# New planned durations and a new order for a planned f32 attention and two-MLP kernel

## The chip, the core and the metric

The kernel runs on one core of a Trainium2 chip. Its engines are TensorE (PE, with weight loads PEld beside it), VectorE (DVE), ScalarE (ACT), GpSimd (POOL) and SyncE (SP), which issues DMAs. The metric is the device time of one execution in microseconds (us).

## The reference

For 4 batches of 12 heads (448 tokens, 64 elements), all in f32:

```python
q_n, k_n = rmsnorm(q, g_q), rmsnorm(k, g_k)          # over head_dim
scores = q_n @ k_n.T / sqrt(64)
attn = exp(scores - max(scores)); attn /= sum(attn) + 1e-9
x = (attn @ v) as [1792, 768]
h = x @ w_in1;  x = (h * sigmoid(1.702 * h)) @ w_out1        # 768 -> 2048 -> 768
h = x @ w_in2;  out = (h * clip(h + 3, 0, 6) / 6) @ w_out2   # 768 -> 2048 -> 768
```

## The kernel before

TensorE has to deliver f32 accuracy, so nearly every operand is cut into a 16-bit "high" part and a 16-bit "low" part, and a product is made of two or three 16-bit products of 128x448. Making these parts is the work of the other engines: `scaled` (L479 ScalarE, L482 VectorE, L485 GpSimd) writes high parts, `rest` (L494, VectorE) and `split` (L509 GpSimd, L510 VectorE) low parts. Weights arrive as f32 and are decoded (L613 to L634) and split too.

The stages overlap. Per batch: squares and root of the norms (L971 to L1018), norm products (L1028), high and low parts of q and k (L1034 to L1049), a transposition by DMA, then per pair of heads seven score tiles in groups of one or two. A score group is a chain over four engines: score products (L1203, L1206) into one of two PSUM buffers `s`, row maxima (L1211, VectorE), their scaling to the exponentials' bias (L1215, ScalarE, 128x2), the exponentials with row sums (L1216, ScalarE), the sums' scaling (L1221, ScalarE, 128x2), the reciprocals (L1224, VectorE). The exponentials release the `s` buffer. In batch 0 the probabilities are scaled through a diagonal matrix (L485 on GpSimd, 128x128) and turned by TensorE (L1265), in the later batches they are split and turned by DMA. The products with v are L1131 (batch 0) and L1164. MLP 1 follows for each batch: inward products L1410 (16 column blocks `f`, 18 products each), gate, L1459 (VectorE), split, then outward products L1478. MLP 2 (seven products in the place of eight: L1654 and L1769) comes last, for all batches.

No loop order is written out. Every operation is recorded in a plan with its dependencies, buffers and its ways: `op([(POOL, ns, f), (DVE, ns, g)], deps)` may run on either engine. `Plan.rank` gives each the longest planned path to the end (plus hand-set offsets `off` and `own`), `Plan.order` then lists all operations by planned start; where there are several ways it takes the engine with the earliest planned end plus a bias (`bias0` in batch 0, `bias1` in batch 1, `bias` after). The planned durations come from small functions such as `t_pe(n) = 0.445 * n`. On the chip each engine runs its own instructions in this fixed order and waits by semaphores; a planned time is only a way to an order. `keep_busy` (L319) puts filler products (L1959, 128x512 bf16, results unused) where the plan sees TensorE idle for longer than `late + idle` ns.

In `add_in` the inward products of `f >= 2` also wait for `kg_ready`, which needs the largest x of the batch (a total over partitions, the TensorE product L444).

Of the kernel before, what the change touches and what calls it, by code (L numbers as in the profile page):

```python
# [9 lines left out]
F16 = mybir.dt.float16  # L10
# [32 lines left out]
    look=[0, 130, 60, 920, 540],  # L43
    off=[-9158, 408922, -29895, 22854, 24586, 19810, -27690, 67476, -181023, 15083, 120686, -34408, -37087, -37194, -689989, -31399, -23083, -347804, 11747, 208998],
    abias=44617,
    cuts=[],
    bias0=[2000, 440, 370, 120, 3040],
    bias1=[8820, 1540, 3900, 3250, 4520],
    dlook=2054,
    warm=9,  # L50
    late=789,
    idle=1000,
    pu=419,
    pmost=5,
# [25 lines left out]
def t_pe(n):  # L80
    return 0.445 * n
# [14 lines left out]
def t_fast(n):  # L96
    return Shared(0.72 * n + 80)


def t_dve_two(n):  # L100
    return Shared(1.04 * n + 150)


def t_dve_rest(n):
    return Shared(1.04 * n + 205)


def t_dve_bits(n):
    return Shared(1.04 * n + 150)


def t_pool(n):
    return Shared(0.78 * n + 290)


def t_pool2(n):
    return Shared(1.5 * n + 380)
# [212 lines left out]
def attention_moe_moe_kernel(ctx, tc, q, k, v, g_q, g_k, w_in1, w_out1, w_in2, w_out2, out):  # L330
# [181 lines left out]

    gp, gq_t = sb.tile([128, D], F32, name="gp"), vr_t[0][:, 0, :]
    gm, ge, tab = small(), small(), small()
    alpha, nalpha = small(), small()
# [4 lines left out]
    SLOTS0 = 10  # L520
    pt0 = carve(arena, 0, [128, 10, 4, 128], F32)

    def constants():
        nc.gpsimd.memset(one, 1.0)
        make_identity(nc, ident)
# [35 lines left out]
    class Weight:  # L561
# [22 lines left out]
        def decoded(self, src, raw, cl):  # L584
# [69 lines left out]
        def add(self, i, m, after):  # L654
# [3 lines left out]
            for j in range(i, i + m):  # L658
# [9 lines left out]
                squares.append(op((ACT, t_act(n, 1) + 45, square), [o] + after))  # L668
# [13 lines left out]
            o = op((DVE, 480 if self.inward else 550, scale), [o], gives=wl)  # L682
# [53 lines left out]
    class Units:  # L736
# [8 lines left out]
        def add(self, q, after, free):  # L745
# [7 lines left out]
            for j in range(2):  # L753
# [63 lines left out]
                squares.append(op((ACT, t_act(n, 1) + 45, square), [o], gives=raw))  # L817
# [71 lines left out]
    msq, rsq, tsq, nbs, zs = small(56), small(56), small(56), small(16), small(16)  # L889
# [53 lines left out]
    def add_norm(bt, after):  # L943
# [75 lines left out]

        def put(n, raw, rooted, gained):  # L1020
# [59 lines left out]
        for grp in groups:  # L1080
# [3 lines left out]
                (DVE, 2300, lambda n=grp[0], m=m: root(n, m)), sum((p[1] for p in parts), [])  # L1084
# [53 lines left out]
    def add_pair(bt, n):  # L1138
# [4 lines left out]
        for p0, j0, t0, m in ((0, 0, 0, 7), (64, 0, 1, 6), (64, 6, 0, 1)):  # L1143
            def load(p0=p0, j0=j0, t0=t0, m=m):
# [3 lines left out]
                128 * m * 256, load, loads[:1] or [bt.vscale] + batches[0].pvs, takes=None if loads else raw_l, wide=False  # L1148
# [20 lines left out]
    def add_units(bt, exp_after, arena_after, x_after):  # L1169
        b = bt.b  # L1170
        bt.xlow, bt.pvs, xmax = [], [], []
        x_factor = 2.0 ** -14 if b else bt.xf
        nslots = 12 if b else SLOTS0
        reads = [arena_after] * nslots
        ring = 0
        u = 0
        rows = lambda h: slice(64 * h, 64 * h + 64)
        for n in range(NP):
            groups = [(0, 1), (2, 3), (4, 5), (6,)] if n % 2 == 0 else [(0,), (1, 2), (3, 4), (5, 6)]
            slots = [(ring + i) % nslots for i in range(7)]  # L1180
            ring += 7
            turns = [None] * 7
# [6 lines left out]
            for grp in groups:  # L1189
                m = len(grp)  # L1190
                sl, pl, hl = Lease(s_ring, m), [Lease(p_ring) for _ in grp], Lease(phl_ring) if b else None
# [21 lines left out]
                def exps(i, sl=sl, nb=nb, z=z, p=p, m=m):  # L1213
                    if i == 0:
                        nc.scalar.activation(out=nb, in_=nb, func=AF.Copy, scale=nalpha)  # L1215
                    nc.scalar.activation(  # L1216
                        out=p(i), in_=s_t[sl.slot][:, i, :S], func=AF.Exp, bias=nb[:, i:i + 1],
                        scale=alpha, accum_out=z[:, i:i + 1],
                    )
                    if i == m - 1:  # L1220
# [786 lines left out]
```

## Time and profile before

| | us |
|---|---|
| median of 3 runs (lowest, highest) | 1145.58 (1145.24, 1148.97) |
| the profiled execution | 1147.63 |
| its span | 1145.8 |
| TensorE busy | 1065.3 (93%) |
| VectorE busy | 822.5 (72%) |
| ScalarE busy | 721.3 (63%) |
| GpSimd busy | 365.1 (32%) |

In the profile's strip of 40 slices TensorE stands at 8 or 9 tenths everywhere but at the start (3) and in one stretch at 129 to 193 us (6, 4 and 4 tenths), and the granted clock falls there to 5 tenths. VectorE stands at 7 to 9 tenths up to there. The DMA engines move 156 GB/s on average. A window of the trace gives for each engine its busy us in that stretch; a row of waits names the engine and line that waited and the instruction whose end released it.

### The profile page before, as it was taken

The numbers are of one execution on the slowest core, as the hardware profiler recorded it, in microseconds if no ns is written. First come the engines' busy times: TensorE is split into PE (matmuls) and PEld (weight loads), VectorE is DVE, ScalarE is ACT, GpSimd is POOL, SyncE is SP. The second block draws the span as 40 slices with busy tenths as digits, with TensorE's granted clock in tenths as the row PEclk, the third lists the DMA queues.
The fourth block names the chain that finished last, engine by engine and source line by source line (L and its number), as shares of the span: only waits on it lengthen the run. The fifth ranks groups of instructions, "written<-read, shape, count | busy, mean of one in ns | idle before, by whom it ended". The sixth has DMA issues, their size and how long they took to land. (4 is left out here: it accounts for less than half of the span.)

```text
span 1145.8 us, 18018 instructions
## 1 busy us (share of the span) xinstructions
PE 1065.3 (93%) x6571; PEld 588.7 (51%) x6571; DVE 822.5 (72%) x1445; ACT 721.3 (63%) x1505; POOL 365.1 (32%) x335
## 2 busy tenths in 40 slices
PE   3888964999999999999999999999999999999998
PEld 1566531554554555545555555555555555555555
DVE  7998889998699764797756878594577455935342
ACT  5999758999868996578885646463565132512210
POOL 6764555353156201350001255552132103200000
PEclk9999985999999999999999999999999999999999
DMA  8977578999976997569895327633451151222033
GB/s 239 193 199 192 167 203 212 204 191 222 241 227 187 173 176 155 181 194 166 171 185 154 120 78 264 231 108 120 146 189 55 56 169 40 71 72 98 1 90 104
DMA packets 236712, 178.88 MB, mean 156 GB/s; under 512 B 194896, under 2 KB 220496, under 8 KB 235088
## 3 DMA queue, kind: packets, MB, share of 16 engines
q1 hardware_dynamic: 236624, 177.74, 59.4%
q8 instruction: 51, 0.84, 0.3%
q14 instruction: 37, 0.30, 0.1%
HBM read 97.88 MB, written 34.41 MB: 115 GB/s over the span
## 5 line engine op out<-in xcount | busy, mean ns | idle before, releaser
L1410 PE MATMUL mm<-xt,wa 128*128 128x448 f16 x1152 | 229.5, 357 | 7.0 <-DVE st L1459 6.8
L1478 PE MATMUL mm<-gt,wb 128*128 128x448 f16 x1152 | 226.7, 352 | 0.7 <-DVE wb L494 0.5
L1769 PEld LDWEIGHTS <-gt 128*128 128x128 f16 x1344 | 131.4, 98 | 92.3 <-issue 4.8
L1410 PEld LDWEIGHTS <-wa 128*128 128x128 f16 x1152 | 113.9, 100 | 114.3 <-issue 14.5
L1478 PEld LDWEIGHTS <-wb 128*128 128x128 f16 x1152 | 111.8, 99 | 103.9 <-issue 1.1
L1654 PEld LDWEIGHTS <-xt 128*128 128x128 f16 x1008 | 98.6, 98 | 93.7 <-issue 3.8
L1216 ACT ACTIVATE p<-s,smalls 128x448 f32<-128x448 f32 x168 | 120.7, 720 | 7.5 <-DVE p L494 3.4
L1654 PE MATMUL s<-wa,xt 128*128 128x448 f16 x576 | 114.1, 352 | 2.1 <-DVE st L1669 2.1
L1211 DVE TENSOR_REDUCE smalls<-s 128x2 f32<-128x896 f32 (+1 forms) x96 | 91.5, 963 | 4.1 <-PE s L1206 3.9
L494 DVE SCALAR_TENSOR_TENSOR p<-p,smalls 128x448 f16<-128x448 f32 x108 | 78.1, 752 | 22.4 <-ACT p L479 22.1
L1203 PE MATMUL s<-gt 128*128 128x448 f16 (+1 forms) x192 | 62.2, 370 | 30.2 <-ACT p L1216 28.3
L1654 PE MATMUL mm<-wa,xt 128*128 128x448 f16 x432 | 86.9, 352 | 0.9 <-ACT wb L1676 0.9
L479 ACT ACTIVATE p<-p,smalls 128x448 f16<-128x448 f32 (+2 forms) x120 | 75.8, 666 | 11.7 <-DMA xt<-p 8.6
L1769 PE MATMUL mm<-p,gt 128*128 128x384 f16 x384 | 72.0, 326 | 0.0
L1769 PE MATMUL mm<-gt 128*128 128x384 f16 x372 | 68.2, 326 | 0.0
L1206 PE MATMUL s<-gt 128*128 128x448 f16 (+1 forms) x192 | 61.9, 366 | 0.0
L1769 PE MATMUL s<-p,gt 128*128 128x384 f16 x288 | 56.1, 326 | 2.4 <-ACT wb L1805 1.2
L1769 PE MATMUL s<-gt 128*128 128x384 f16 x300 | 55.9, 326 | 1.0 <-DVE st L1669 0.6
L494 DVE SCALAR_TENSOR_TENSOR gt<-st,smalls,gt 128x448 f16<-128x448 f32 x64 | 52.4, 829 | 6.1 <-ACT gt L479 4.9
L1808 DVE SCALAR_TENSOR_TENSOR wb<-mm,smalls,wb 128x384 f32<-128x384 f32 x47 | 27.0, 611 | 41.0 <-PE mm L1769 41.0
L479 ACT ACTIVATE gt<-st,smalls 128x448 f16<-128x448 f32 x49 | 32.1, 661 | 29.9 <-DVE st L1459 26.2
L1265 PE MATMUL mm<-gt,p 128*128 128x128 f32 x336 | 44.1, 280 | 6.3 <-DVE xt L1276 1.9
(216 smaller groups left out, 1827.4 us busy)
## 6 DMA issues: line engine op xcount, KB each, us to landing
wr<-in_moe_w_in_dram SPq DMA_DIRECT2D x32, 768.0 KB, 4.9
wa<-park_x SPq DMA_DIRECT2D x21, 672.0 KB, 4.0
wr<-in_moe_w_out_dram SPq DMA_DIRECT2D x12, 1024.0 KB, 6.4
wr<-in_moe_w_out_dram SPq DMA_DIRECT2D x16, 768.0 KB, 4.7
qkd<-xt SPq DMA_DIRECT2D x18, 672.0 KB, 4.7
p<-in_v_dram SPq DMA_DIRECT2D x42, 224.0 KB, 4.1
x2d<-st SPq DMA_DIRECT2D x24, 224.0 KB, 3.1
park_x<-wa SPq DMA_DIRECT2D x2, 2688.0 KB, 13.0
```

What stands on the lines that cost most here:

```text
L479: nc.scalar.activation(out=dst(), in_=src(), func=AF.Copy, scale=s)
L494: nc.vector.scalar_tensor_tensor(out=dst(), in0=src(), scalar=s, in1=high(), op0=ALU.mult, op1=ALU.subtract)
L1203: nc.tensor.matmul(o, lhsT=x[:, 64 * t:64 * t + m], rhs=x[:, 448:896], start=True, stop=False)
L1206: nc.tensor.matmul(o, lhsT=x[:, 64 * t:64 * t + m], rhs=x[:, 896:1344], start=False, stop=True)
L1211: nc.vector.tensor_reduce(out=nb, in_=s_t[sl.slot][:, :m, :S], axis=AX.X, op=ALU.max)
L1216: nc.scalar.activation(out=p(i), in_=s_t[sl.slot][:, i, :S], func=AF.Exp, bias=nb[:, i:i + 1], scale=alpha, accum_out=z[:, i:i + 1],)
L1265: nc.tensor.matmul(mm_t[tl.slot][:, 128 * j:128 * j + 128], lhsT=p(i)[:, c:c + 128], rhs=diag(), start=True, stop=True,)
L1410: nc.tensor.matmul(mm_t[ml.slot][:, :n], lhsT=w.inw(we, kc, f), rhs=x[:, xe, kc, :n], start=(kc == k0 and i == 0), stop=(kc == k1 - 1 and ...
L1478: nc.tensor.matmul(mm_t[ml.slot][:, :S], lhsT=W2.outw(we, fc, d * 128, 128), rhs=gv[:, ge_, fc, :], start=(fc == g.part.start and i == 0), ...
L1654: nc.tensor.matmul(self.bank(k), lhsT=w[:, we, fa, kc], rhs=xs[:, fb, xe, kc], start=first and kc == 0 and j == 0, stop=kc == 2 and j == 2 ...
L1769: nc.tensor.matmul(mm_t[banks[h].slot][:, :half], lhsT=g[:, ge, f, tb * 128:tb * 128 + 128], rhs=w4_t[part % 2][:, f, we, h * half:h * hal ...
L1808: nc.vector.scalar_tensor_tensor(out=view(), in0=bank(), scalar=self.co, in1=view(), op0=ALU.mult, op1=ALU.add)
```

## The change

The arithmetic of the output is the same. Changed are the numbers that the plan goes by, and a few operations' ways.

- Planned durations: TensorE products 0.445 to 0.4225 ns a column, the total over partitions 420 to 150, the batch-0 products with v 2400 to 4290; the fast VectorE form 0.72n+80 to 0.57n+75, VectorE's two-input, `rest` and 16-bit forms 55 to 72 ns shorter, GpSimd's two-input form 120 ns shorter; some scalings longer.
- The scalings at L1215 and L1221 are no longer part of the exponentials' operation. Each is an operation of its own with three ways, ScalarE, GpSimd or VectorE (L1280, L1282, L1284 and L1295, L1297, L1299 of the new file).
- The root of the norms gets a way on GpSimd; the new order never takes it. New code for `plain` and `defer` is there, with values that leave the old computation; one small memset is added.
- All tuning numbers (`bias`, `off`, `own`, `late` 789 to 500, `idle` 1000 to 900, ...) are new, so the order is planned anew.

```diff
-    bias0=[2000, 440, 370, 120, 3040],
-    bias1=[8820, 1540, 3900, 3250, 4520],
+    bias0=[10940, 1120, 970, 600, 5420],
+    bias1=[8440, 0, 13700, 2530, 6480],
-    late=789,
-    idle=1000,
+    late=500,
+    idle=900,
...
 def t_pe(n):
-    return 0.445 * n
+    return 0.4225 * n
 def t_fast(n):
-    return Shared(0.72 * n + 80)
+    return Shared(0.57 * n + 75)
 def t_dve_two(n):
-    return Shared(1.04 * n + 150)
+    return Shared(1.04 * n + 80)
 def t_pool2(n):
-    return Shared(1.5 * n + 380)
+    return Shared(1.5 * n + 260)
...
-        o = op((PE, 420, emit), deps, takes=lease)
+        o = op((PE, 150, emit), deps, takes=lease)
...
-                    if i == 0:
-                        nc.scalar.activation(out=nb, in_=nb, func=AF.Copy, scale=nalpha)
...
+                o = op([
+                    (ACT, 265, lambda nb=nb, late=late: nc.scalar.activation(
+                        out=nb, in_=nb, func=AF.Copy, scale=nalpha, bias=UP if late else 0.0)),
+                    (POOL, 510, lambda nb=nb, late=late: nc.gpsimd.tensor_scalar(
+                        out=nb, in0=nb, scalar1=nalpha, scalar2=UP if late else 0.0, op0=ALU.mult, op1=ALU.add)),
+                    (DVE, 150, lambda nb=nb, late=late: nc.vector.tensor_scalar(
+                        out=nb, in0=nb, scalar1=nalpha, scalar2=UP if late else 0.0, op0=ALU.mult, op1=ALU.add)),
+                ], [o])
...
-                        (ACT, t_act(S, 3) + 200 * (i == 0) + 160 * (i == m - 1), lambda i=i, f=exps: f(i)),
+                        (ACT, t_act(S, 1 if late else 3) - 35, lambda i=i, f=exps: f(i)),
...
-                o = op((PE, 12 * t_pe(S) + 700, both_heads), deps[0] + deps[1] + vdone, takes=ml, gives=vl)
+                o = op(
+                    (PE, (19 if late else 12) * t_pe(S), both_heads), deps[0] + deps[1] + vdone,
+                    takes=[ml, zl] if late else ml, gives=vl,
+                )
...
-                o = op((PE, 2400, both), deps[0] + deps[1], takes=ml, gives=vls[0])
+                o = pv_done = op((PE, 4290, each_head), deps[0] + deps[1], takes=ml, gives=vls[0])
```

What the new order does is read at three places. The new file's lines are 10 to 91 higher: L1071, L1092, L1089, L504, L1261, L1501, L454 and L2050 are before's L1028, L1049, L1046, L494, L1216, L1410, L444 and L1959.

The first is VectorE in the norms of batch 1, before:

```order
L494 SCALAR_TENSOR_TENSOR gt<-p,smalls,gt 128x7x64
L1028 TENSOR_TENSOR xt<-xt,smalls 128x448 x2
L494 SCALAR_TENSOR_TENSOR gt<-p,smalls,gt 128x7x64
L1046 TENSOR_TENSOR xt<-xt 128x7x64
L1049 TENSOR_TENSOR xt<-xt 128x7x64
L459 TENSOR_SCALAR smalls<-mm_74 128x1
```
and now:

```order
L1071 TENSOR_TENSOR xt<-xt,smalls 128x448 x2
L1092 TENSOR_TENSOR xt<-xt 128x7x64
L1071 TENSOR_TENSOR xt<-xt,smalls 128x448
L1089 TENSOR_TENSOR xt<-xt 128x7x64 x2
L504 SCALAR_TENSOR_TENSOR gt<-p,smalls,gt 128x7x64
L1092 TENSOR_TENSOR xt<-xt 128x7x64
```
Norm products and low parts (`xt` on both sides) that GpSimd did before stand here on VectorE.

The second is ScalarE in the first score groups of batch 0 (`s` is the score buffer, `smalls` holds maxima and sums), before:

```order
L1215 ACTIVATE smalls<-smalls 128x2
L1216 ACTIVATE p,smalls<-s_75,smalls 128x448 x2
L1221 ACTIVATE smalls<-smalls 128x2
L479 ACTIVATE gt<-gt,smalls 128x128
L613 ACTIVATE wr<-wr 128x768
L1034 ACTIVATE gt<-wb 128x896
L1275 COPY xt<-mm_73 128x512
L1215 ACTIVATE smalls<-smalls 128x2
L1216 ACTIVATE p,smalls<-s_76,smalls 128x448
```
ScalarE now, without the 128x2 rows:

```order
L1261 ACTIVATE p,smalls<-s_75,smalls 128x448 x2
L685 ACTIVATE wa,smalls<-wb 128x6x128
L1261 ACTIVATE p,smalls<-s_76,smalls 128x448 x2
L685 ACTIVATE wa,smalls<-wb 128x6x128
L1261 ACTIVATE p,smalls<-s_75,smalls 128x448 x2
L946 ACTIVATE p,smalls<-p 128x448
L1261 ACTIVATE p,smalls<-s_76,smalls 128x448
```
and GpSimd at the same place, where the rows L1282 and L1297 are those scalings:

```order
L495 TENSOR_SCALAR gt<-wb 128x7x64
L1089 TENSOR_TENSOR gt<-wb,gt 128x7x64
L1282 TENSOR_SCALAR smalls<-smalls 128x2
L1092 TENSOR_TENSOR gt<-wb,gt 128x7x64
L1282 TENSOR_SCALAR smalls<-smalls 128x2
L1297 TENSOR_SCALAR smalls<-smalls 128x2
L495 TENSOR_SCALAR gt<-gt,smalls 128x128
L1297 TENSOR_SCALAR smalls<-smalls 128x2
L495 TENSOR_SCALAR gt<-gt,smalls 128x128 x2
```
They are queued between the large parts of k and q (`gt<-wb`) and the diagonals (L495).

The third is TensorE in batch 0's inward products, where the total that `f >= 2` waits for is made, before (`mm` are PSUM tiles, `wa` the weights):

```order
L1410 MATMUL mm_71<-xt,wa 128x448
L1410 LDWEIGHTS wa
L1410 MATMUL mm_71<-xt,wa 128x448
L444 MATMUL mm_74<-smalls 128x1
L1410 LDWEIGHTS wa
L1410 MATMUL mm_72<-xt,wa 128x448
```
and now, where the pair of L2050 stands 58 times in a row, and the inward products of `f >= 2` behind it:

```order
L1501 LDWEIGHTS wa
L1501 MATMUL mm_72<-xt,wa 128x448
L454 MATMUL mm_73<-smalls 128x4
L2050 LDWEIGHTS ident_70
L2050 MATMUL mm_74<-ident_70 128x512
```
Where TensorE's queue went straight on to the next column block, fillers stand now. In the whole program the fillers go from 36 to 124. By the order, VectorE has 1580 instructions (1447 before), ScalarE 1150 (1207), GpSimd 278 (340); GpSimd has 53 of the 192 small scalings (44 of them before the first outward product of batch 0), VectorE 10. Before the first outward product of batch 0, TensorE has 170 score products where it had 156.

## Rows read from the trace of the kernel before

**Rows 1.** Windows: busy us of each engine by stretch, granted clock; they overlap.
```profile
core 0: us, PE busy (x) PEld busy (x) DVE busy (x) ACT busy (x) POOL busy (x), PEclk, DMA share, GB/s
0.00:25.00 25.00, 5.51 (x14) 2.04 (x15) 17.05 (x41) 13.00 (x28) 14.59 (x22) 1.00 0.80 229
25.00:238.00 213.00, 174.87 (x1149) 105.37 (x1150) 194.65 (x355) 182.52 (x421) 123.00 (x119) 0.93 0.79 199
129.00:193.00 64.00, 37.49 (x182) 17.54 (x181) 56.02 (x108) 44.80 (x87) 35.41 (x29) 0.78 0.77 211
238.00:316.00 78.00, 73.77 (x528) 39.94 (x527) 62.05 (x125) 72.17 (x164) 25.61 (x23) 1.00 0.92 218
316.00:722.00 406.00, 398.29 (x2514) 209.20 (x2513) 303.50 (x540) 296.62 (x659) 123.74 (x111) 1.00 0.72 176
722.00:1146.00 424.00, 412.89 (x2375) 232.16 (x2373) 245.25 (x386) 156.96 (x237) 78.19 (x63) 1.00 0.31 100
```

**Rows 2.** Waits of TensorE from 129 to 193 us: total, times, longest.
```profile
PE s L1203 <- ACT p L1216: 14.7, 4, 4.9
PE mm L1410 <- DVE st L1459: 6.5, 2, 5.8
PE mm L444 <- ACT p L1216: 5.1, 1, 5.1
```

**Rows 3.** VectorE by line and shape, 0 to 238 us: count, busy us, mean ns.
```profile
L1211 DVE TENSOR_REDUCE smalls<-s 128x2 f32<-128x896 f32 x28 | 29.9, 1077 | 0.1
...
L494 DVE SCALAR_TENSOR_TENSOR p<-p,smalls 128x448 f16<-128x448 f32 x13 | 12.7, 996 | 0.5 <-ACT p L479 0.5
...
L634 DVE SCALAR_TENSOR_TENSOR wr<-wr 128x1024 int32<-128x1024 int32 x6 | 8.8, 1464 | 0.3 <-ACT wr L613 0.3
...
L1028 DVE TENSOR_TENSOR xt<-xt,smalls 128x448 f32<-128x448 f32 x5 | 5.1, 1060 | 0.0
L494 DVE SCALAR_TENSOR_TENSOR wb<-wr,smalls,wb 128x1024 f16<-128x1024 f32 x4 | 5.1, 1269 | 0.0
L628 DVE TENSOR_SCALAR wr<-wr 128x1024 uint16<-128x1024 uint16 x6 | 4.5, 743 | 0.0
...
L1046 DVE TENSOR_TENSOR xt<-xt 128x448 f16<-128x448 f32 x2 | 2.1, 1034 | 0.0
...
L510 DVE TENSOR_TENSOR p<-p 128x448 f16<-128x448 f32 x1 | 1.4, 1449 | 0.0
```

**Rows 4.** Timeline of VectorE from 147 to 150 us: start, duration.
```profile
147.73 1.15 DVE L1028 TENSOR_TENSOR xt<-xt,smalls 128x448 f32<-128x448 f32 x2
148.80 0.68 DVE L494 SCALAR_TENSOR_TENSOR gt<-p,smalls,gt 128x448 f16<-128x448 f32 x1
149.40 0.62 DVE L1046 TENSOR_TENSOR xt<-xt 128x448 f16<-128x448 f32 x1
```

**Rows 5.** GpSimd by line and shape, 0 to 238 us.
```profile
L485 POOL TENSOR_SCALAR gt<-gt,smalls 128x128 f32<-128x128 f32 x28 | 17.4, 626 | 22.5 <-DVE smalls L1224 16.7 <-PE mm L1265 4.8 <-ACT wa L479 0.6
...
L1028 POOL TENSOR_TENSOR xt<-xt,smalls 128x448 f32<-128x448 f32 x7 | 7.5, 1093 | 5.7 <-DVE smalls L1018 5.7
...
L524 POOL MEMSET smalls<- 128x1 f32 x1 | 0.1, 98 | 0.3 <-POOLq L1980 0.3
```

**Rows 6.** ScalarE by line and shape, 0 to 238 us.
```profile
L1215 ACT ACTIVATE smalls<-smalls 128x2 f32<-128x2 f32 x28 | 8.0, 286 | 4.7 <-DVE smalls L1211 4.7
...
L1221 ACT ACTIVATE smalls<-smalls 128x2 f32<-128x2 f32 x27 | 5.5, 204 | 0.9
```

**Rows 7.** Timeline of TensorE from 130 to 242 us.
```profile
135.33 6.97 PE L1410 MATMUL mm<-xt,wa 128*128 128x448 f16 x36
...
192.87 8.55 PE L1410 MATMUL mm<-xt,wa 128*128 128x448 f16 x36
...
237.80 4.51 PE L1478 MATMUL mm<-gt,wb 128*128 128x448 f16 x23
```

**Rows 8.** Waits of TensorE from 238 us to the end.
```profile
PE s L1654 <- DVE st L1669: 2.1, 1, 2.1
```

More of the change, by code (lines that the diff above doesn't have):

```diff
@@ L511, in split, with pieces_of @@
         ], [x], gives=gives)
+    def pieces_of(dst, src, n, deps, takes=None, gives=None):
+        hi, lo = (lambda: dst(0)), (lambda: dst(1))
+        x = op(scaled(hi, src, 1.0, n), deps, takes=takes)
+        return x, op([
+            (POOL, t_pool2(n), lambda: nc.gpsimd.tensor_tensor(out=lo(), in0=src(), in1=hi(), op=ALU.subtract)),
+            (DVE, t_dve_two(n), lambda: nc.vector.tensor_tensor(out=lo(), in0=src(), in1=hi(), op=ALU.subtract)),
+        ], [x], gives=gives)
     gp, gq_t = sb.tile([128, D], F32, name="gp"), vr_t[0][:, 0, :]
     gm, ge, tab = small(), small(), small()
-    alpha, nalpha = small(), small()
+    alpha, nalpha, ones = small(), small(), small(32).bitcast(F16)
     flat = vhl.rearrange("p t e d -> p (t e d)").bitcast(F32)
@@ L524, in constants @@
         nc.gpsimd.memset(one, 1.0)
+        nc.gpsimd.memset(ones, 1.0)
         make_identity(nc, ident)
@@ L1083, in add_norm @@
             rooted = op(
-                (DVE, 2300, lambda n=grp[0], m=m: root(n, m)), sum((p[1] for p in parts), [])
+                [(DVE, 2450, lambda n=grp[0], m=m: root(n, m)), (POOL, 4400, lambda n=grp[0], m=m: root_pool(n, m))],
+                sum((p[1] for p in parts), []),
             )
@@ L1136, in add_head0, with add_pair @@
         return product, deps + loads, raw_l
-    def add_pair(bt, n):
+    def add_pair(bt, n, after):
         raw_l, vl = Lease(pair_ring, 2), Lease(vhl_ring)
@@ L1147, in add_pair @@
             loads.append(sp(
-                128 * m * 256, load, loads[:1] or [bt.vscale] + batches[0].pvs, takes=None if loads else raw_l, wide=False
+                128 * m * 256, load, loads[:1] or [bt.vscale] + batches[0].pvs + after, takes=None if loads else raw_l, wide=False
             ))
@@ L1171, in add_units @@
         bt.xlow, bt.pvs, xmax = [], [], []
[L1172 to L1175, printed above, removed]
+        plain_pvs = []
         u = 0
@@ L1179, in add_units @@
             groups = [(0, 1), (2, 3), (4, 5), (6,)] if n % 2 == 0 else [(0,), (1, 2), (3, 4), (5, 6)]
+            plain = n < CFG['plain'][b]
+            late = not plain and n < CFG['defer'][b]
+            if n in (0, CFG['plain'][b]):
+                nslots, ring = SLOTS0 if plain else 12, 0 if plain else 7 * (n % 2)
+                reads = [arena_after + plain_pvs] * nslots
             slots = [(ring + i) % nslots for i in range(7)]
             ring += 7
+            x_factor = bt.xf if plain else 2.0 ** -14
             turns = [None] * 7
@@ L1299, in xhigh, with xlow @@
                 )
-            def xlow(ml, r, high=high, low=low):
+            def xlow(ml, r, high=high, low=low, x_factor=x_factor):
                 nc.vector.scalar_tensor_tensor(
@@ L1335, in add_units @@
-                if early:
-                    def put(n=n, both=both):
-                        queue().dma_start(
-                            out=xd[b % 2][n], in_=both().rearrange("p e c -> p (e c)")
-                        )
-                    def get(n=n):
-                        queue().dma_start(
-                            out=xt[:, :, n, :], in_=xd[b % 2][n].rearrange("p (e c) -> p e c", e=2)
-                        )
-                    early.left = 2
-                    sq.also.append(early)
-                    x = sp(128 * 1792, put, [x], gives=early)
-                    x = sp(128 * 1792, get, [x] + x_after, wide=False)
@@ L1350, in add_units @@
-                bt.xlow.append(x)
+                    if zl:
+                        for r in range(max(len(x) for x in runs)):
+                            for i in range(7):
+                                for h in range(2):
+                                    if r < len(runs[h]):
+                                        c, q0, m, s, w = runs[h][r]
+                                        nc.tensor.matmul(
+                                            mm_t[zl.slot][64 * h:64 * h + 64, c:c + m * w], lhsT=ones,
+                                            rhs=pt[:, s:s + w, i, q0:q0 + m], start=i == 0, stop=i == 6,
+                                        )
@@ L1351, in add_units, with each_head @@
+                o = op(
+                    (PE, (19 if late else 12) * t_pe(S), both_heads), deps[0] + deps[1] + vdone,
+                    takes=[ml, zl] if late else ml, gives=vl,
+                )
+                pv_done = o
+                if late:
+                    o = op((ACT, t_act(S), offset), [o], takes=ql, gives=zl)
+                    o = op((DVE, 2 * t_dve(S) + 60, divide), [o], gives=ql)
             else:
-                ml = Lease(mm_ring)
                 products, deps, vls = zip(*ready)
-                def both(ml=ml, products=products):
+                def each_head(ml=ml, products=products):
@@ L1445, in add_in @@
                 m = lambda f=f: half(f)
-            o = op((ACT, t_act(n, 2) - 50, lambda f=f, t=t, m=m: gate(f, t(), m())), [o, ready[group(f)]], takes=pl)
+            o = op((ACT, t_act(n, 2) - 110, lambda f=f, t=t, m=m: gate(f, t(), m())), [o, ready[group(f)]], takes=pl)
             o = op((DVE, t_dve(n), lambda t=t, m=m: product(t(), m())), [o], gives=None if early else ml)
@@ L1487, in add_out1 @@
                         deps += W2.done[2 * d:2 * d + 2]
-                    last[0] = op((PE, 3 * t_pe(S) + 8, emit), deps, takes=None if fc > g.part.start else ml)
+                    last[0] = op((PE, 3 * t_pe(S), emit), deps, takes=None if fc > g.part.start else ml)
                 def scale(d=d, g=g):
```

150 lines of the change are left out of this document (102 added, 48 removed), and 26 rows, old and new, of the table own.

## Prediction

> **What bounds the kernel now.** Read the windows first [rows 1]. From 238 us on TensorE is busy 398.3 of 406 and 412.9 of 424 us: 7.7 + 11.1 = 18.8 us are all that a better order can return there, beside 4.2 us in 238 to 316. Before 238 us it is busy 5.5 + 174.9 of 238. So what the change is worth is decided up to the first outward product of batch 0, which starts at 237.8 [rows 7]. In the worst stretch, 129 to 193 us, TensorE is busy 37.5 of 64 us at a granted clock of 0.78, VectorE 56.0, ScalarE 44.8, GpSimd 35.4. Then read who ends TensorE's waits there [rows 2]: 14.7 + 5.1 us on the exponentials, 6.5 us on VectorE's gate product. The exponentials look guilty; but ScalarE has 19 us free in that stretch and VectorE 8. The exponentials of one score group wait for VectorE's maxima, which wait in VectorE's queue behind the norms and low parts of batch 1. Up to 238 us VectorE is busy 17.05 + 194.65 = 211.7 us and idle 26.3, of which 25 - 17.05 = 8.0 lie in the start and 18.3 after it. That is the bound I go by: how much work VectorE has in front of the first outward product, and how much idle time stays in it.
>
> **What the change puts on VectorE up to there**, counted in the two orders: 8 norm products (L1028), 4 and 2 low parts (L1046, L1049), 5 of L510, 4 more maxima of two tiles, 4 more `rest` (L494), one W2 slice more; less 0.6 us of three small differences. The cheapest price of each is that of the timeline where it stood alone or nearly so [rows 4]: 1.15 / 2 = 0.57 us for a norm product, 0.62 for a low part (taken for L510 too, same shape), 0.68 for L494. Maxima 1.08; the W2 slice 0.74 + 1.46 + 1.27 = 3.5 [rows 3]. Sum: 8 x 0.57 + 11 x 0.62 + 4 x 0.68 + 4 x 1.08 + 3.5 - 0.6 = 4.6 + 6.8 + 2.7 + 4.3 + 3.5 - 0.6 = 21.3 us. By the means of the whole stretch [rows 3], 1.06, 1.03, 1.45 (L510) and 1.00 (L494), it is 8.5 + 6.2 + 7.3 + 4.0 + 4.3 + 3.5 - 0.6 = 33.2 us. So the added work is between 21.3 and 33.2.
>
> **What it takes away from GpSimd gives some of that back.** The same VectorE form takes 0.57 us in one place [rows 4] and 1.06 in the mean [rows 3]: it is slowed where GpSimd works beside it. GpSimd loses 23 large operations there, some 28 us by its rows (1.09 us each [rows 5] and above), and gets 44 small scalings. If each us of GpSimd slows VectorE by (1.06 - 0.57) / 1.06 = 0.45 us, the relief is 0.45 x 28 = 12.5 us; at worst it is 0, since GpSimd also overlaps maxima and one-input forms, of which no row shows a slowing. I take 5, below the middle, because the 44 scalings come into the same stretch. The Trainium skill ("SBUF — State Buffer", Who interferes with whom) says that a VectorE instruction with two SBUF inputs and a GpSimd one that reads SBUF exclude each other, and the second is held until the first has ended. By that rule the relief is whole, which is the faster rival below; that 0.57 and 1.06 us both occur for the norm product agrees with it, how often the two meet no row tells.
>
> VectorE then has 211.7 + 21.3 - 5 = 228 us up to the first outward product (220.5 to 245). It keeps the 8 us of the start, and of the 18.3 idle us the new order, which interleaves more closely, may leave 2 to 18; I take 10, the middle. 228 + 8 + 10 = 246 us. TensorE has done 14 more score products by then, 14 x 6.97 / 36 = 2.7 us [rows 7], so that no loss would be 237.8 + 2.7 = 240.5. **Term 1: +5.5 us** (from 220.5 + 8 + 2 = 230.5, which is -10, to 271, of which I take +30 as the end).
>
> **Fillers.** 58 of them stand in front of the inward products of `f >= 2`. One is 0.194 x 512 / 448 = 0.22 us by the 128x448 products [rows 7], 58 are 12.8 us. TensorE waited 6.5 us there for VectorE and 5.1 for ScalarE at the total [rows 2]. If their inputs come as late as before, the fillers lie in waiting time up to 11.6 us and cost 1.2; if 5 us earlier, they cost 6. I price them at nothing beyond term 1: it rests on VectorE, which they don't delay.
>
> **Clock.** The fillers keep TensorE at work where it now idles. Thirty-six products take 8.55 us at 192.87, behind the score waits, and 6.97 at 135.33 [rows 7]; the granted clock of 129 to 193 is 0.78 [rows 1], between the two levels. With the gap filled the 1.6 us of that run are saved; the other slowed products lie between waits and save nothing. **Term 2: -1.6** (0 to -3).
>
> **Small scalings.** On ScalarE the two cost 0.286 + 0.204 us a group [rows 6]. Before the first outward product 27 + 27 of two tiles and 10 + 9 of one went off or stayed; 6 exponentials, 4 high parts and 3 decodes come on, so that ScalarE is about even there. On GpSimd one costs at least 0.098 us, the small memset, and at most 0.626, the 128x128 scaling [rows 5]; I take 0.25, nearer the memset, as two columns are nearer to one than to 128. Two of them are then what ScalarE takes, so nothing, beside the extra hop, which the other groups of the ring cover while VectorE is the bound. What is queued behind them on GpSimd are the diagonals, and TensorE's turns wait for those; that is the slower rival.
>
> **From 238 us on.** Between there and the first inward product of batch 1, VectorE gets 11 us less to do and ScalarE 18 less, of 62.1 and 72.2 in 78 us [rows 1]; TensorE's idle 4.2 may halve. **Term 3: -2** (0 to -4). At the switch to MLP 2 the new order puts 6 and 2 fillers in two gaps where before waited 2.1 us [rows 8]: a gap gets fillers only if the plan sees 1.4 us beyond them, so 2 x 1.4 + 8 x 0.22 = 4.6, against 2.1. **Term 4: +2** (-2 to +4, which covers the rest of the late stretches: VectorE gets more and GpSimd less, but TensorE has only 18.8 us of idle there).
>
> **Sum:** 5.5 - 1.6 - 2 + 2 = +3.9 us. The profiled execution took 1147.63, so 1151.5; the median of the runs is 2.05 us lower, and the time is compared with that: 1145.58 + 3.9 = 1149.5 us.
>
> **Rivals.**
> Faster: GpSimd's withdrawal frees VectorE by the whole 12.5 us and the idle closes to 2. For it: VectorE's forms at 1.06 against 0.57 us; against it: each score group's chain still needs all engines in turn, so VectorE idles at each hop. Then term 1 is -10, and 1145.6 - 10 - 1.6 - 2 + 2 = 1134 us (1128 to 1142).
> No change: the two engines' loads are only exchanged; VectorE keeps its 18 idle us less what it has to add, and term 1 lies between -3 and +2. 1146 us (1142 to 1149).
> Slower, one mechanism: the small scalings on GpSimd lengthen the score chain. A scaling stands there behind a part of k or q of 1.1 to 1.4 us, as the order shows; ScalarE would have taken it at once in 0.29. Of some 22 groups with such a scaling before 238 us, each waits half of 1.1 us more, twice (maximum and sum): 22 x 1.1 = 24 us of chain, of which the two `s` buffers hide about half: +12 on top of term 1 without its idle half: 1145.6 + 3.9 + 10 = 1159 us (1153 to 1168). It decides once the queue ahead of a scaling on GpSimd is longer than the 0.5 us that ScalarE took for both. For it: TensorE's longest waits are those on the exponentials [rows 2]. Against it: GpSimd is free for 28 us more.
>
> **Chances.** Forecast 0.38 (1145 to 1156; 0.15 of it within the bound of no change), faster rival 0.33, no change 0.16, slower rival 0.13. About 0.3% (3.4 us) is what a measurement of this kernel can tell from no change: 1142.2 to 1149.0. Faster: nearly the whole rival and a little of the forecast's and of no change's lower edges, 0.34. Same: 0.13 + 0.15 = 0.28. Slower: 0.25 - 0.01 of the forecast, above 1149, and 0.13: 0.38 rounded. The range holds 0.8 if it reaches from 1133, which leaves out some 0.13 of the faster rival, to 1162, which leaves out 0.05 of the slower one. My forecast's own range is 1145 to 1156.
>
> **What would show it.** VectorE's busy time up to the first outward product (228 forecast) and its idle time there (18); the start of that product (246 forecast, 230 for the faster rival); the norm product's mean on VectorE, 1.06 now: near 0.6 speaks for the whole relief. The granted clock around the 58 fillers near 1. TensorE's waits on the exponentials in batch 0: longer, with GpSimd's small scalings started well after the maxima, shows the slower rival. The idle of TensorE from there on near 20 us. The forecast is wrong if the first outward product starts before 240 us, or if TensorE's idle after it changes by more than 5 us.

## Result and profile after

The changed kernel takes 1158.26 us (1156.05 to 1159.84, 4 runs) against 1146.66 us for the kernel before on the same chips (4 runs): a ratio of 1.0097, interval 1.0074 to 1.0119. It is slower by 11.6 us, where 3.9 were forecast.

The windows of the changed kernel, with the columns of [rows 1]; 250.5 us is the first outward product of batch 0, 325.3 the first inward product of batch 1:

```profile
core 0: us, PE busy (x) PEld busy (x) DVE busy (x) ACT busy (x) POOL busy (x), PEclk, DMA share, GB/s
0.00:250.50 250.50, 199.68 (x1263) 116.93 (x1264) 223.96 (x433) 198.31 (x426) 125.07 (x168) 0.94 0.79 196
129.00:193.00 64.00, 53.00 (x248) 24.83 (x249) 61.19 (x123) 47.27 (x91) 26.24 (x24) 0.89 0.88 235
193.00:238.00 45.00, 35.18 (x252) 19.20 (x250) 39.85 (x76) 40.01 (x90) 11.46 (x13) 0.89 0.84 177
...
0.00:325.30 325.30, 270.99 (x1771) 157.61 (x1772) 285.61 (x559) 258.02 (x555) 147.20 (x185) 0.95 0.80 202
325.30:1156.00 830.70, 810.19 (x4890) 440.98 (x4887) 562.18 (x1020) 449.72 (x880) 92.22 (x89) 1.00 0.51 136
```

and of the kernel before, up to its own first inward product of batch 1 at 316.0 us and from there on:

```profile
0.00:237.80 237.80, 180.18 (x1160) 107.31 (x1161) 211.51 (x395) 195.32 (x446) 137.38 (x140) 0.94 0.79 202
0.00:316.00 316.00, 254.15 (x1688) 147.36 (x1689) 273.75 (x519) 267.69 (x610) 163.20 (x162) 0.95 0.82 206
316.00:1146.00 830.00, 811.19 (x4887) 441.36 (x4885) 548.76 (x926) 453.58 (x895) 201.93 (x174) 1.00 0.51 137
193.00:238.00 45.00, 44.37 (x302) 23.75 (x301) 42.41 (x70) 40.59 (x92) 20.66 (x17) 0.97 0.89 194
```

Read the rows that start at 325.3 and 316.0 first. From that inward product on both kernels need 830 us: nearly the whole difference, 9.3 of the spans' 9.9 us, has arisen before it. Up to there VectorE is busy 285.6 us instead of 273.8, and idle 39.7 instead of 42.2. ScalarE and GpSimd have less to do than before (258.0 against 267.7, 147.2 against 163.2). (In 129 to 193 us the strip of the kernel before has two low slices, 6 and 4 tenths, and not three.) The timeline of TensorE shows where the time falls due:

```profile
136.25 12.68 PE L2050 MATMUL mm<-ident 128*128 128x512 bf16 x58
148.77 6.41 PE L1501 MATMUL mm<-xt,wa 128*128 128x448 f16 x33
...
187.52 9.32 PE L1501 MATMUL mm<-xt,wa 128*128 128x448 f16 x36 [0.85 <-DVE st L1550]
...
204.00 4.70 PE L1501 MATMUL mm<-xt,wa 128*128 128x448 f16 x24
...
219.24 0.59 PE L454 MATMUL mm<-smalls 128*128 128x1 f32 x2 [5.33 <-ACT wb L685]
223.31 2.40 PE L1501 MATMUL mm<-xt,wa 128*128 128x448 f16 x6 [3.49 <-DVE st L1550]
...
250.50 3.00 PE L1569 MATMUL mm<-gt,wb 128*128 128x448 f16 x15
```

Counted by products, the new kernel is level with the old one at 204 us (174 inward products against 172, 132 score products against 128). Between 213 and 223 us TensorE then stands still (idle 9.8 us in 193 to 238, 0.6 before). Its queue is at the total of a W2 slice, which waits for a square on ScalarE, and behind that at an inward block whose PSUM buffers VectorE has not released.

VectorE's two-input operations after, against [rows 3], up to 250 us:

```profile
L1071 DVE TENSOR_TENSOR xt<-xt,smalls 128x448 f32<-128x448 f32 x9 | 7.6, 885 | 0.0
L1071 DVE TENSOR_TENSOR wb<-wb,smalls 128x448 f32<-128x448 f32 x6 | 6.6, 1101 | 0.0
L1089 DVE TENSOR_TENSOR xt<-xt 128x448 f16<-128x448 f32 x6 | 3.7, 655 | 0.0
L520 DVE TENSOR_TENSOR p<-p 128x448 f16<-128x448 f32 x6 | 3.7, 614 | 0.0
```

There are more of them, and most are cheaper than before (0.89 for 1.06 us, 0.66 for 1.03, 0.61 for 1.45), but not the norm products on `wb`: 1.10 us, where the two of the kernel before took 0.98. The small scalings on GpSimd, in the groups by line up to 247 us:

```profile
L495 POOL TENSOR_SCALAR gt<-gt,smalls 128x128 f32<-128x128 f32 x30 | 17.6, 589 | 8.7 <-PE mm L1328 3.5 <-DVE smalls L1267 3.2 <-DVE smalls L1284 0.7
...
L1282 POOL TENSOR_SCALAR smalls<-smalls 128x2 f32<-128x2 f32 x14 | 8.9, 636 | 4.8 <-DVE smalls L1258 3.1 <-DVE smalls L1267 1.2
...
L1297 POOL TENSOR_SCALAR smalls<-smalls 128x2 f32<-128x2 f32 x19 | 6.0, 314 | 6.3 <-ACT p L1261 5.6
```

In the mean two columns take 0.64 and 0.31 us there, more than on ScalarE in [rows 6]. The last section shows what these means are made of.

### The profile page after: what moved, and what is told of

The parts are those of the page before. It is cut to its first block, busy times and chain, and to the rows that moved or that the text cites. A ratio compares the mean times of both kernels' runs of the same rounds, so it can differ in the third digit from the quotient of the medians.

```text
span 1155.7 us, 18078 instructions
## 1 busy us (share of the span) xinstructions
PE 1081.2 (94%) x6659; PEld 598.6 (52%) x6659; DVE 847.8 (73%) x1578; ACT 707.7 (61%) x1435; POOL 239.4 (21%) x273
## 4 chain that ended last, share of the span: by engine, by line
PE 72%; DVE 17%; ACT 4%; issue 3%; DMA 3%; POOL 2%; SPq 0%; ACTq 0%; DVEq 0%; POOLq 0%
PE mm L1569 16%; PE mm L1501 12%; PE mm L1860 9%; PE s L1860 9%; PE s L1745 8%; PE mm L1745 6%; PE mm L1208 4%; PE s L1250 2%; PE mm L1328 2%; PE s L1253 2%; DVE smalls L1258 2%; DMA p<-in_v_dram 1%; DVE smalls L995 1%; DVE xt L1071 1%; ACT p L1261 1%
## 5 line engine op out<-in xcount | busy, mean ns | idle before, releaser
L1501 PE MATMUL mm<-xt,wa 128*128 128x448 f16 x1152 | 230.1, 357 | 9.5 <-DVE st L1550 9.4
L1501 PEld LDWEIGHTS <-wa 128*128 128x128 f16 x1152 | 113.8, 100 | 116.4 <-issue 16.6
L1261 ACT ACTIVATE p<-s,smalls 128x448 f32<-128x448 f32 x168 | 120.2, 718 | 16.3 <-DVE p L504 6.0
L1745 PE MATMUL s<-wa,xt 128*128 128x448 f16 x549 | 109.4, 352 | 3.2 <-DVE st L1760 1.7
L1745 PE MATMUL mm<-wa,xt 128*128 128x448 f16 x459 | 92.7, 352 | 0.8 <-ACT wb L1767 0.8
L504 DVE SCALAR_TENSOR_TENSOR p<-p,smalls 128x448 f16<-128x448 f32 x108 | 75.7, 728 | 18.0 <-ACT p L489 17.8
L1860 PE MATMUL mm<-p,gt 128*128 128x384 f16 x384 | 79.5, 326 | 0.0
L1250 PE MATMUL s<-gt 128*128 128x448 f16 (+1 forms) x192 | 61.5, 364 | 18.2 <-ACT p L1261 11.9
L1860 PE MATMUL s<-gt 128*128 128x384 f16 x348 | 75.1, 326 | 2.9 <-DVE wb L1899 1.8
L1860 PE MATMUL mm<-gt 128*128 128x384 f16 x324 | 70.9, 326 | 0.0
L1860 PE MATMUL s<-p,gt 128*128 128x384 f16 x288 | 63.7, 326 | 3.7 <-DVE st L1760 1.1
L1899 DVE SCALAR_TENSOR_TENSOR wb<-s,smalls,wb 128x384 f32<-128x384 f32 x42 | 24.8, 614 | 43.9 <-PE s L1860 42.6
L1208 PE MATMUL mm<-xt,gt 128*64 128x64 f16 (+3 forms) x858 | 48.5, 261 | 2.9 <-DVE st L1550 2.9
## 6 DMA issues: line engine op xcount, KB each, us to landing
p<-in_v_dram SPq DMA_DIRECT2D x41, 224.0 KB, 4.5
x2d<-st SPq DMA_DIRECT2D x24, 224.0 KB, 2.2
```

What stands on the lines that cost most here:

```text
L504: nc.vector.scalar_tensor_tensor(out=dst(), in0=src(), scalar=s, in1=high(), op0=ALU.mult, op1=ALU.subtract)
L1208: nc.tensor.matmul(mm_t[ml.slot][64 * h:64 * h + 64, c:c + m * w], lhsT=vhl[:, 2 * (i % 4) + i // 4, part], rhs=pt[:, s:s + w, i, q0:q0 + ...
L1250: nc.tensor.matmul(o, lhsT=x[:, 64 * t:64 * t + m], rhs=x[:, 448:896], start=True, stop=False)
L1261: nc.scalar.activation(out=p(i), in_=s_t[sl.slot][:, i, :S], func=AF.Exp, bias=nb[:, i:i + 1], scale=alpha, accum_out=None if late else z[ ...
L1501: nc.tensor.matmul(mm_t[ml.slot][:, :n], lhsT=w.inw(we, kc, f), rhs=x[:, xe, kc, :n], start=(kc == k0 and i == 0), stop=(kc == k1 - 1 and ...
L1745: nc.tensor.matmul(self.bank(k), lhsT=w[:, we, fa, kc], rhs=xs[:, fb, xe, kc], start=first and kc == 0 and j == 0, stop=kc == 2 and j == 2 ...
```

## Experiments

Four theories: L, VectorE's work sets the pace up to batch 1; O, the order by itself holds TensorE up at 213 to 223 us; S, the small scalings on GpSimd; F, the fillers. Later ones are named in the expectations. All times are medians of 4 runs (9 for e10); the ratio is to the kernel before, run beside them (1145.86 us for e1 to e4, 1144.51 for e5 to e8, 1146.68 for e9 to e12). The table gives for each profiled run the first inward product of batch 1, and VectorE until then; the sections refer to it.

| kernel | us | batch 1's first inward product | VectorE busy | idle |
|---|---|---|---|---|
| before | 1146.7 | 316.0 | 273.8 | 42.2 |
| after | 1158.3 | 325.3 | 285.6 | 39.7 |
| e1 after's order, before's engines | 1183.6 | 338.8 | 279.9 | 58.9 |
| e2 small scalings on ScalarE | 1158.7 | 327.9 | 284.9 | 43.0 |
| e3 without the long fillers | 1158.7 | 325.6 | 286.3 | 39.3 |
| e4 before's order, after's engines | 1179.8 | 338.6 | 278.3 | 60.3 |
| e5 gates early, total late | 1160.8 | 327.5 | 285.2 | 42.3 |
| e6 gates early only | 1160.9 | 326.7 | 285.9 | 40.8 |
| e7 before, new durations | 1173.5 | 337.0 | 284.6 | 52.4 |
| e8 after, old durations | 1219.2 | 339.1 | 293.4 | 45.7 |
| e9 before, more on VectorE | 1159.1 | 326.5 | 288.9 | 37.6 |
| e10 after, less on VectorE | 1150.8 | 318.1 | 274.1 | 44.0 |
| e11 after, two-input ops back | 1163.3 | 331.3 | 281.8 | 49.5 |
| e12 before, two-input ops moved | 1153.1 | 319.9 | 275.7 | 44.2 |

### e1 and e4: the order and the engines, crossed

The operations of the two kernels match one to one apart from the small scalings, so either order can be run with the other's choice of engines (`WAYS` lists the engine of each operation that differs; e4 also has the small scalings on after's engines, inside the exponentials' operation):

```diff
         for o in self.done:
-            o.way[2]()
+            e = WAYS.get(getattr(o, 'key', -1))
+            way = next((w for w in o.ways if w[0] == e), o.way) if e is not None else o.way
+            way[2]()
```

> The changed kernel's order, but every operation on the engine that it had before (336 operations move back, the small scalings all go to ScalarE, the 13 loads back to SyncE's queue). Theory L (the prediction's: VectorE's added work): the loss goes, 1146 to 1150 us, first outward product of batch 0 near 240 us. Theory O (the new order holds TensorE up by itself, at the total that waits for a square and at the late gates around 213 to 223 us): 1155 to 1160 us, first outward product near 250 us. Theory S (small scalings on GpSimd): 1147 to 1150. Theory F (fillers): 1157.

> The kernel before with its own order, but every operation on the engine that the change gives it (276 operations and 63 small scalings move; the loads stay). Theory L: the loss appears here, 1153 to 1160 us. Theory O: 1145 to 1149 us, as before. Theory S: 1153 to 1158, with longer waits of TensorE on the exponentials in 25 to 129 us. Theory F: 1147.

e1 took 1183.62 us (1.033, 1.0314 to 1.0346), e4 1179.77 (1.0307, 1.0287 to 1.0327). Both mixtures are far slower than either whole kernel, so no theory was right: neither the order nor the engines alone carries the loss, each serves the other. In both, VectorE has less to do than in the changed kernel, and its idle time until batch 1 grows to 59 and 60 us. TensorE in 193 to 238 us, e1 and then e4:

```profile
193.00:238.00 45.00, 31.75 (x193) 16.61 (x193) 41.89 (x76) 37.51 (x83) 17.11 (x16) 0.89 0.92 206
```
```profile
193.00:238.00 45.00, 32.59 (x185) 15.60 (x185) 42.86 (x78) 39.74 (x87) 15.02 (x14) 0.78 0.82 202
```

### e2 and e3: small scalings and fillers

e2 sets `WAYS` for the 63 small scalings alone. e3:

```diff
-        for _ in range(n):
+        for _ in range(n if n < 20 else 0):
```

> The changed kernel's order and engines, but its 63 small scalings of GpSimd and VectorE are put on ScalarE, at their places in the order. Theory S: the score chains of batch 0 get shorter, 1148 to 1152 us. Theories L, O and F: no difference within 3 us (1155 to 1161), since the new kernel is level with before at 200 us, where all score chains of batch 0 are over.

> The changed kernel without its two long runs of fillers (58 and 21 of the 124). Theory F (the 58 hold up inward products that are ready at 136 us): up to 12 us earlier there, 1147 to 1152 us. Theories L, O and S: the products come earlier and then wait longer for VectorE; 1156 to 1161, the granted clock of 129 to 193 us falls from 0.89 to about 0.8.

1158.69 us (1.0116, 1.0101 to 1.0131) and 1158.70 (1.0113, 1.0093 to 1.0132): no difference from the changed kernel. Theories S and F fall. In e3 the granted clock of 129 to 193 us drops as expected,

```profile
129.00:193.00 64.00, 41.83 (x180) 19.27 (x180) 60.97 (x123) 47.54 (x92) 27.54 (x24) 0.79 0.81 234
```

to 0.79 from 0.89 (means over stretches at the full level, 2.4 GHz, and at the half one), with TensorE busy 11 us less, VectorE as busy as in the changed kernel, and not one us lost. The run takes away the fillers and the clock together; TensorE's timeline in e3 shows why neither counts:

```profile
139.97 5.25 PE L1501 MATMUL mm<-xt,wa 128*128 128x448 f16 x18 [3.27 <-DVE smalls L469]
150.50 4.89 PE L1501 MATMUL mm<-xt,wa 128*128 128x448 f16 x15 [5.28 <-DVE st L1550]
```

The inward products start at 139.97 us, where the fillers held them to 148.77, and then wait for VectorE's gate product. The next score products come at 155.5 us in e3 and at 155.1 in the changed kernel.

### e5 and e6: the stall at 213 to 223 us

`MOVE` emits operations behind another one in the order: three gates with their products and parts, and in e5 also two inward blocks, and the total behind them.

```diff
+        moved = {k for ks in MOVE.values() for k in ks}
+        by = {getattr(o, 'key', -1): o for o in self.done}
         for o in self.done:
+            if getattr(o, 'key', -1) in moved:
+                continue
             o.way[2]()
+            for k in MOVE.get(getattr(o, 'key', -1), ()):
+                by[k].way[2]()
```

> The changed kernel with three gates of batch 0's MLP 1 (and their products and parts) 10 to 20 us earlier in the queues of ScalarE and VectorE, the two column blocks behind them earlier on TensorE, and the total of a W2 slice, at which TensorE stands until 219 us, behind these blocks. Theory O (the order at 213 to 223 us holds TensorE up): the 9 us of idle time there fall to 2 or 3, first outward product near 244 us instead of 250.5, 1149 to 1154 us. Theory L (VectorE's and ScalarE's work sets the pace): the idle time comes back within 30 us, first outward product 248 to 251, 1156 to 1160 us.

> The same three gates earlier, TensorE's queue as in the changed kernel. Theory O: TensorE still stands at the total until 219 us and only its next wait of 3.5 us goes, 1154 to 1157 us. Theory L: 1156 to 1160 us, no difference from the changed kernel.

1160.84 us (1.013, 1.0091 to 1.0169) and 1160.91 (1.0127, 1.0098 to 1.0157). Theory O falls. The repair does what it should and gains nothing, as TensorE's timeline in e5 shows (L1518 are inward, L1267 score products):

```profile
214.07 6.97 PE L1518 MATMUL mm<-xt,wa 128*128 128x448 f16 x36
...
223.96 0.38 PE L471 MATMUL mm<-smalls 128*128 128x1 f32 x2 [2.92 <-ACT wb L702]
...
228.82 0.53 PE L1267 MATMUL s<-gt 128*128 128x448 f16 x1 [4.48 <-ACT p L1278]
231.77 0.53 PE L1267 MATMUL s<-gt 128*128 128x448 f16 x1 [2.05 <-ACT p L1278]
```

The two blocks now run at 214 us, and 10 us later TensorE waits 6.5 us for exponentials instead; in 193 to 238 us it is idle 11.9 us, after 9.8 in the changed kernel. The place of a stall is not the cause of the loss.

### e7 and e8: the planned durations alone

e7 sets the change's durations (such as those in the diff above) in the kernel before, e8 those of before in the changed kernel, each with its own tuning numbers.

> The kernel before, planned anew with the change's planned durations alone: its own tuning numbers, small scalings still inside the exponentials. Theory D (durations nearer to the measured ones make the better order by themselves): 1140 to 1150 us. Theory T (the hand-set offsets fit one set of durations, and any other set spoils the order): 1160 to 1185 us.

> The changed kernel, with its tuning numbers and small scalings of their own, but planned with the durations of before. Theory D: slower than the changed kernel because of the worse durations, 1160 to 1170 us. Theory T: 1165 to 1190 us, as far off as the other mixture.

1173.46 us (1.0237, 1.0213 to 1.0262) and 1219.20 (1.0641, 1.0612 to 1.067). Theory D falls. e7 lies in the range of theory T, e8 29 us above it: durations and offsets that were not set together spoil the order. The new durations buy nothing here by themselves. In e7 the first outward product starts at 235.0 us, earlier than before's 237.8; the 21 us are lost from there to batch 1 (102.0 us for 78.2), with 155 fillers in the program instead of 36, and what these fillers cost was not run. e8 loses 36 us more than any other kernel behind the first inward product of batch 1. The timelines of e8 show where (L454 are totals):

```profile
753.07 0.16 DVE L469 TENSOR_SCALAR smalls<-mm 128x1 int32<-128x1 int32 x1 [39.51 <-PE mm L454]
...
754.39 8.58 PE L2050 MATMUL mm<-ident 128*128 128x512 bf16 x39
762.83 0.38 PE L454 MATMUL mm<-smalls 128*128 128x1 f32 x2
763.08 25.41 PE L2050 MATMUL mm<-ident 128*128 128x512 bf16 x117
788.33 1.87 PE L1745 MATMUL s<-wa,xt 128*128 128x448 f16 x9
```

At the switch to MLP 2 TensorE runs 156 fillers, 34 us, where the changed kernel has 8. VectorE, which stood idle for 39.5 us until a total on TensorE ended at 753 us, is busy 33.2 us of these 34 with the parts that the products of MLP 2 need. In e8's order TensorE has nothing but fillers and a total in this stretch.

### e9 and e10: VectorE's load, more and less

e9, in the kernel before, for batch 0 (`first`):

```diff
-            gdone.append(op(rest(lo, t, s, hi, n), [o], gives=pl))
+            low = rest(lo, t, s, hi, n)
+            if first:
+                low = (low[0], low[1], lambda f=low[2]: (f(), f()))
+            gdone.append(op(low, [o], gives=pl))
```

e10, in the changed kernel:

```diff
-                    nc.vector.tensor_reduce(out=ms[:, TB * i:TB * i + TB], in_=sq(i), axis=AX.X, op=ALU.add)
+                    nc.vector.tensor_reduce(
+                        out=ms[:, TB * i:TB * i + TB], in_=sq(i)[:, :, :16] if b == 1 else sq(i), axis=AX.X, op=ALU.add
+                    )
...
-                    nc.vector.tensor_reduce(out=nb, in_=s_t[sl.slot][:, :m, :S], axis=AX.X, op=ALU.max)
+                    nc.vector.tensor_reduce(out=nb, in_=s_t[sl.slot][:, :m, :S // 2 if b == 1 else S], axis=AX.X, op=ALU.max)
```

> The kernel before with the low part of each gated column block of batch 0 computed twice on VectorE (15 more operations of 0.68 to 0.87 us before the first outward product, 10 to 13 us, off the score chain; the output does not change). Theory L (VectorE's work sets the pace there, one for one): first outward product at 247 to 250 us, 1154 to 1158 us. Theory H (hops between the engines set the pace, and VectorE's idle 26 us take the work in): first outward product below 242 us, 1144 to 1149 us.

> The changed kernel with shorter reductions on VectorE in batch 1: the sums of squares over 16 of 64 elements (12 x about 0.4 us) and the maxima over 224 of 448 columns (14 x 0.5 + 4 x 0.25 us), some 13 us less VectorE work before the first outward product; the output of batch 1 is another. Theory L: first outward product at 238 to 242 us, 1146 to 1150 us. Theory H: 246 to 251 us, 1154 to 1159 us, only the score chains get a little shorter.

e9 took 1159.05 us (1.0113, 1.009 to 1.0136), e10 1150.75 (1.0039, 1.0027 to 1.0052). Up to batch 1's first inward product, e9 and then e10:

```profile
0.00:326.50 326.50, 258.51 (x1687) 147.96 (x1688) 288.88 (x537) 268.49 (x610) 162.29 (x162) 0.94 0.78 200
```
```profile
0.00:318.10 318.10, 267.87 (x1771) 156.55 (x1772) 274.11 (x559) 257.44 (x555) 147.42 (x185) 0.96 0.80 207
```

Work for VectorE that is not in the score chains costs the kernel before 12 us: VectorE is busy 15 us longer, batch 1 comes 10.5 us later. 11.5 us less in the changed kernel bring batch 1 7.2 us forward and the end 7.5. VectorE's idle time takes up the rest (37.6 and 44.0 against 42.2 and 39.7). So theory L holds in the main, not one for one but at 0.69 (e9) and 0.63 us (e10) for one us of VectorE, and e9, whose first outward product came at 246.6 us, rules theory H out for the kernel before. e9's end is 1 us above the range that L gave it. e10 is less clear: its end is 0.75 us above L's range and below H's, and its first outward product, at 246.7 us, came later than L expected and lies in H's range. Up to there VectorE is busy 8.8 us less than in the changed kernel, and the product comes 3.8 us earlier:

```profile
0.00:246.70 246.70, 197.88 (x1263) 117.21 (x1264) 215.16 (x435) 198.36 (x427) 124.64 (x169) 0.95 0.78 199
```

Its shorter maxima also shorten the score chains, so the share of load in its gain is not measured apart.

### e11 and e12: the two-input operations alone

`WAYS` for 31 of them (25 one way, 6 the other), in the changed kernel and in the kernel before.

> The changed kernel with only its two-input operations (norm products, gains, low parts, before the first outward product) on the engines that had them before: 25 from VectorE to GpSimd, 6 the other way. Theory L without contention: VectorE has 11 us less, 1147 to 1151 us. Theory X (the two engines exclude each other in these operations, so nothing is won by the move): 1156 to 1161 us. Theory T (an order serves only the engines it was planned for): 1163 us and more.

> The kernel before with these 31 operations on the engines that the change gives them. Theory L without contention: VectorE has 11 us more, 1153 to 1157 us. Theory X: 1144 to 1149 us. Theory T: 1155 us and more, by longer waits of TensorE with VectorE's idle time grown, not shrunk.

e11 took 1163.34 us (1.0148, 1.0127 to 1.0169), e12 1153.10 (1.0064, 1.0039 to 1.009). Up to the first outward product of batch 0, e12 and then e11:

```profile
0.00:240.40 240.40, 181.43 (x1160) 108.62 (x1161) 212.56 (x411) 194.99 (x444) 115.28 (x123) 0.91 0.77 198
```
```profile
0.00:256.20 256.20, 201.23 (x1262) 117.03 (x1263) 221.02 (x413) 199.24 (x425) 143.98 (x187) 0.93 0.75 191
```

In e12 VectorE takes over 19 operations net until batch 1, 17 of them before the first outward product: some 10 us at 0.6 us each, an estimate from [rows 4]. It is busy 1.1 us more than before up to there (212.6 against 211.5); GpSimd is busy 22 us less. So VectorE's operations became some 9 us cheaper, 0.4 us for each us of GpSimd; its rows with the same count in both runs fell by 6.8 us, 0.31 for each. e11 shows the same from the other side: 11 us of work go back, VectorE is busy 3 us less, and its rows with the same count rose by 8.4 us, 0.44 for each of GpSimd's 19 us. The load is nearly as theory X says. But X's times don't hold: with hardly more load, e12 is 6.4 us slower than before, which lies in L's range without L's load; its profiled run shows 3.9 at the first inward product of batch 1, with 2 us more VectorE work and 2 more idle. e11, with less work on VectorE than the changed kernel, is slower than it, as theory T has it, and VectorE is idle 49.5 us. That the rest of e12's loss is T's too, an order not planned for these engines, is argued and not shown.

## Why the prediction was right in direction and short in size

The direction was little more than luck: slower had a chance of 0.38, faster 0.34. The time, 1158.26 us, lies outside the forecast's own range of 1145 to 1156 us. The bound was a right one: VectorE's load moves the end in both kernels (e9, e10), though e1, e4 and e11 show that it is not the only thing that does. VectorE's work in front of the first outward product was forecast at 228 us and measured at 224.0; the stages from batch 1's inward products on were forecast unchanged within 4 us and are (830.4 against 829.8 us).

The step that failed is "of the 18.3 idle us the new order, which interleaves more closely, may leave 2 to 18; I take 10, the middle". VectorE's idle time up to the first outward product was 26.5 us, and 26.3 before: nothing closed. In e9 and e10 11 to 15 us more or less work until batch 1 change it by only 4 or 5. That it comes from the hops of the score chains between the engines, which are as many as before, is argued and not shown. With 18 instead of 10 kept, the forecast would have been 228 + 8 + 18 = 254; the product started at 250.5; that the work came out 4 us lower hid part of the error. So **term 1**, with the extra score products taken off, was 250.5 - 240.5 = +10 us and not +5.5.

**The relief by GpSimd** was taken at 5 us, with 0.45 us for each of GpSimd's us as the most (by the prediction's own numbers 0.46, which changes nothing). By e12 and e11 it is 0.31 to 0.44: two thirds of that most and more. That fits the Trainium skill's rule ("SBUF — State Buffer", Who interferes with whom) that such operations of the two engines exclude each other. In the trace of after, the 28 decode operations that were L634, with 82 `rest` and 28 of L628, take 8.6 us less up to batch 1 than before, at the same counts. By the sign that the prediction named, norm products near 0.6 us, the relief is still not whole: they took 0.89 and 1.10. And GpSimd's withdrawal was 12.3 us up to the first outward product (137.4 to 125.1), not 28, since the small scalings took 18 us there. The relief did not make the kernel faster, because other work came in up to batch 1: norm products and low parts 15 us, roots of norms about 5, small and 128x128 scalings 4.7; the last two are not in the prediction's list.

**Term 2**, -1.6 for the clock, was nothing: in e3 the clock falls again, without the fillers, and the time stays. The run of 36 products that was to get back from 8.55 to 6.97 us took 9.32, at 187.52 us. **Fillers** at nothing was right, for the stated reason. **Term 3**, -2: from the first outward product to batch 1's first inward product it took 74.8 us instead of 78.2, of which 2.7 are the score products already done, so -0.7; ScalarE had 12.7 us less to do there (59.7 for 72.4), but VectorE, which was to have 11 less, had 0.6 (61.7 for 62.3). **Term 4**, +2, was +0.6 (1155.7 - 325.3 = 830.4 us of span left, against 1145.8 - 316.0 = 829.8). Together 10 - 0 - 0.7 + 0.6 = +9.9, the difference of the spans.

**The rivals.** The faster one was nearer in its first half (more relief than 5 us) and failed in its second (idle closed to 2). The slower one named a mechanism that is not there: e2 takes the small scalings off GpSimd and gains nothing, though the two together cost twice what was estimated (0.64 and 0.31 us in the mean, against 0.25 each), and TensorE's waits on the exponentials in 129 to 193 us fell from 19.8 to 1.2 us. That its time, 1159 us, was nearly measured is chance.

Open is how the loss of 12 us divides between VectorE's extra work and the pairing of order and engines. By e9's rate (10.5 us for 15.1) the 11.8 us more of VectorE work come to 8 of the 9.3 us at batch 1, but no run has this extra work taken out of the changed kernel with all else as it was. The change also issues 13 loads of v from ScalarE's queue instead of SyncE's; e1 puts them back together with all else, and no run does so by itself.

## What to carry to other kernels

When a list scheduler decides the order, find the engine whose work before the next full stage plus a steady idle time gives that stage's start, and price a new plan by that engine's work; don't credit the plan with closing idle time that no run has shown to close. Repairing the one place where TensorE stands still, giving up the fillers and the clock there, or shortening a chain that isn't the pace changed nothing in four experiments here. Planned durations, offsets and engine choices form one fit in these two kernels: each mixture of their parts that was run is slower than the kernel before.

## What the runs showed of the hardware

- The means of GpSimd's small scalings, 0.64 us for 128x2 by a value per partition and 0.31 with constants, hide two cases. Of the 44 before the first outward product, of two columns or one, 31 took 0.19 to 0.27 us, no more than ScalarE's 0.29 and 0.20. The 13 others took 0.47 to 1.44 us. Each of these began while VectorE ran an operation with two inputs from SBUF, the on-chip memory (L655, L504), or a 16-bit one (L649), and ended within 0.14 us of it or of the next such operation; beside a reduction or a copy from PSUM they were short. From both timelines of the changed kernel:

```profile
32.54 0.94 DVE L655 SCALAR_TENSOR_TENSOR wb<-wr,wb 128x768 int32<-128x768 int32 x1
32.73 0.89 POOL L1282 TENSOR_SCALAR smalls<-smalls 128x2 f32<-128x2 f32 x1 [0.21 <-DVE smalls L1258]
...
36.92 1.09 DVE L1258 TENSOR_REDUCE smalls<-s 128x2 f32<-128x896 f32 x1
37.66 0.19 POOL L1297 TENSOR_SCALAR smalls<-smalls 128x2 f32<-128x2 f32 x1 [0.70 <-ACT p L1261]
```

- A us of GpSimd cost VectorE 0.31 us (e12) to 0.44 us (e11) in the operations that both runs have alike. Norm products on VectorE fell from 1.06 to 0.74 us in e12, where 25 of GpSimd's two-input operations had moved away and 6 come in:

```profile
L1034 DVE TENSOR_TENSOR xt<-xt,smalls 128x448 f32<-128x448 f32 x9 | 6.3, 743 | 0.0
```

- A granted clock of 0.79 instead of 0.89 over 64 us in which TensorE waits for VectorE, with 79 fillers fewer, changed the time by less than the runs vary (e3).
